# Weight loads on another queue, v ahead of them, and weight conversions placed between attention steps in a two-block kernel

## The chip, the cores and the metric

The kernel runs on one NeuronCore of a Trainium2 chip. The metric is device time in microseconds of one execution; several executions are timed and the median is given. A separate execution is recorded by the hardware profiler, and its span is slightly shorter than the timed value. Engine names are those of the profile: PE (TensorE matmul), PEld (its weight loads), DVE (VectorE), ACT (ScalarE), POOL (GpSimd), SP (SyncE, which here only issues transfers).

## The reference

Two blocks follow each other. The first is a gated recurrence per batch and head, the second a gated state-space block on its output. All inputs are float32 except where the harness hands over 64-bit floats for the weights; the kernel reads the weights as pairs of 32-bit words.

```python
# attention: B=4, H=8, S=768, D=48
for t in range(S):
    state = alpha[:, :, t, :, None] * state + einsum('bhd,bhe->bhde', k[:, :, t], v[:, :, t])
    y[:, :, t] = einsum('bhd,bhde->bhe', q[:, :, t], state)
x = y.transpose(0, 2, 1, 3).reshape(B, S, H * D)      # 384 wide
# second block: d_inner = 512
proj = x @ w_in                                        # 384 x 1024
val, gate = proj[..., :512], proj[..., 512:]
h = exp(A_log) * h + val[:, t]                         # scan over t
out = (silu(gate) * h) @ w_out                         # 512 x 384
```

## The kernel before

The function `fast` does the work; a second function, `general`, only runs if checks of the input ranges fail, and takes no part in the times. The sequence is cut into 12 groups of 256 rows (three for each of four batches), and each group into two chunks of 128. A group passes through two parts.

**Attention part.** Alpha is brought to a transposed layout (`natural_alpha` for the first three groups: PE transposes, ACT copies into `aT`). `products` scans alpha on DVE into cumulative products and their inverses. `natural_qk` transposes k and q on PE, and `times` multiplies them on DVE by inverse and product, into Z. `scores` are matmuls of Z with Z, `masks` multiplies them with a triangular mask (one half on DVE, the other copied by ACT and multiplied on POOL, tile A), `keys` transposes k back for the state. `state` accumulates the state of the recurrence in PSUM and ACT copies it to `S_sb`; `values` and `carried` make the output y from A and v, and from the state and Z. `join` copies y to xT on ACT and moves 16 rows of each head pair to their place by six small transfers within SBUF.

**Second part.** `project` makes, for each of four blocks of 128 inner channels, pv and pg from xT and `w_in`: six matmuls, each into a PSUM tile of a pool of three (`ps_mm`), which transposes and outputs share. `gated` scans pv on DVE into hh, applies Silu to pg on ACT (sg), and multiplies both on POOL (f). `output` multiplies f with `w_out`, and SP stores the result.

**Weights.** They arrive as two 32-bit words for each element. `load_w_in(half, engine)` loads half of w_in into partitions 64 x half and up, in two transfers (48 rows and 16 rows, 1152 and 384 KB). `load_w_out` takes two transfers of 768 KB. `convert(i)` turns the words into float32: ACT makes `wr` from the low words, DVE two operations from the high words, and the returned function adds wr on POOL. The first four conversions are the four blocks of w_in (each needs both halves of the load); conversions NI and NI + 1 are the two halves of w_out. The wr tiles come from a pool of two buffers.

**Order.** The program is written out by hand: each engine runs its instructions in the order in which the code issues them, and waits only on semaphores of what it needs. Transfers are issued from SP, ACT or POOL, each with a queue of its own in the profile: q1 is SP's, q10 is ACT's, q0 (named software_dynamic) is POOL's. In the prologue SP issues, in this order, alpha, k and q of group 0, alpha of group 1, v of group 0, k and q of group 1, half 0 of w_in, v of group 1, w_out, and then the inputs of groups 2 and 3. ACT issues half 1 of w_in after the copies of group 0's masks. Group 0 and group 1 go through attention before the main loop; the loop then projects group n while it computes attention of group n + 1 and the products of n + 2. For group 0 (`nat` is true only there) the two conversions of w_out stand after the second and the third projection.

The lines that matter around the change: L443 (transfers of w_in), L448 (w_out), L429 (v), L510 (wr on ACT), L511 and L513 (conversion on DVE), L515 (add on POOL), L557 (aT), L652 (mask on POOL), L685 and L688 (state and S_sb), L664 and L675 (values and carried), L698 (transfers of join), L713 (projection), L720, L725, L726 (hh, sg, f), L734 (output). Between the attention of group 1 and the loop, the code reads:

```python
    for i in range(NI):
        convert(i)()
    state(1, 0)
    values(1, 0)
    values(1, 1)
    state(1, 1)
    carried(1, 0)
    carried(1, 1)
    join(1, (nc.gpsimd, nc.gpsimd))
```

Of the kernel before, what the change touches and what calls it, by code (L numbers as in the profile page):

```python
# [346 lines left out]
def fast(  # L347
# [22 lines left out]
    C = 128  # L370
# [10 lines left out]
    def pool(name, bufs, **kw):  # L381
        return ctx.enter_context(tc.tile_pool(name=name, bufs=bufs, **kw))
# [2 lines left out]
    p1 = pool("p1", 1)  # L385
    p2 = pool("p2", 2)
    p3 = pool("p3", 3)
    ps_sc = pool("ps_sc", 2, space=PS)
    ps_st = pool("ps_st", 1, space=PS)
    ps_mm = pool("ps_mm", 3, space=PS)  # L390
# [35 lines left out]
    def load_v(m, engine, cs=range(G)):  # L426
        b, g = divmod(m, NG)
        for c in cs:
            engine.dma_start(out=vs[m % NV][:, c, :, 0:D],  # L429
                             in_=v[b, :, ds(g * GC + c * C, C), :].rearrange("h p d -> p h d"))  # L430
# [9 lines left out]
    def load_w_in(half, engine):  # L440

        for row, size, first, step in ((64 * half, D, 4 * half * D, D), (64 * half + D, R, (4 * half + 3) * D, R)):
            engine.dma_start(out=bits_in[ds(row, size)].rearrange("p kk n two -> p kk (n two)"),  # L443
                             in_=moe_w_in.bitcast(U32)[ds(first, NK * step)]
                             .rearrange("(kk p) n -> p kk n", p=step)[0:size])
# [51 lines left out]
    def convert(i):  # L497


        if i < NI:  # L500
            bits = bits_in.rearrange("p kk (vg n) two -> p kk vg n two", vg=2)[:, :, :, ds(i * C, C)]
            w = w_in[:, :, :, ds(i * C, C)]
        else:
            rows = ds(2 * (i - NI), 2)
            bits, w = bits_out[:, rows, None], w_out[:, rows, None, :]
        lo, hi = bits[..., 0], bits[..., 1]
        _, x, y, z = w.shape
        r = p2.tile([C, x, y, z], I32, tag="wr", name="wr")
        t = w.bitcast(U32)
        nc.scalar.activation(r, lo, AF.Copy, scale=2.0 ** -29)  # L510
        nc.vector.tensor_scalar(out=t, in0=hi, scalar1=3, scalar2=0x3FFFFFFF,  # L511
                                op0=ALU.logical_shift_left, op1=ALU.bitwise_and)
        nc.vector.scalar_tensor_tensor(out=t, in0=hi, scalar=0xC0000000, in1=t,  # L513
                                       op0=ALU.bitwise_and, op1=ALU.bitwise_or)
        return lambda: nc.gpsimd.tensor_tensor(out=w.bitcast(I32), in0=w.bitcast(I32), in1=r, op=ALU.add)  # L515
# [35 lines left out]
    def natural_alpha(m):  # L551

        for c in range(G):
            tp = ps_mm.tile([C, 4, C], FP32, tag="mm", name="tn")
            for p in range(4):
                nc.tensor.transpose(tp[:, p, :], natural("a", m)[:, c, 2 * p:2 * p + 2, :], ident)
            nc.scalar.activation(alphas[:, :, ds(c * C, C)], tp, AF.Copy)  # L557

    def natural_qk(m, name):

        if m not in Zs:
            Zs[m] = p2.tile([C, 4, 2, GC], FP32, tag="Z", name="Z")
        tps = []
        for c in range(G):
            tp = ps_sc.tile([C, 4, C], FP32, tag=f"sc{c}", name="tn")
            for p in range(4):
                nc.tensor.transpose(tp[:, p, :], natural(name, m)[:, c, 2 * p:2 * p + 2, :], ident)
            tps.append(tp)

        def times(c):  # L570
            i, by = {"k": (1, invs), "q": (0, prods)}[name]
            cols = ds(c * C, C)
            nc.vector.tensor_mul(Zs[m][:, :, i, cols], tps[c], by[:, :, cols])  # L573
        return times

    def check_alpha(m):

        if m < NAT:
            src = natural("a", m)[:, :, :, 0:D]
        else:  # L580
            src = raw_bufs[m % NR]["a"].rearrange("p h (j d) -> p h j d", d=D)[:, :, :, 0:32]
        _, x, y, z = src.shape
        junk = p1.tile([C, x, y, z], BF16, tag="junk", name="junk")
        nc.scalar.activation(junk, src, AF.Relu, bias=minus, accum_out=above[:, m:m + 1])
# [53 lines left out]
    def scores(m, c):  # L638
        Z = Zs[m]
        cols = ds(c * C, C)  # L640
        sc = [ps_sc.tile([C, 4, C], FP32, tag=f"sc{i}", name=f"sc{i}") for i in range(2)]
        for p in range(4):
            for i in range(2):
                rows = ds(64 * i, D)
                nc.tensor.matmul(sc[i][:, p, :], Z[rows, p, 1, cols], Z[rows, p, 0, cols], start=True, stop=True)  # L645
        As[m, c] = p2.tile([C, 2, 4, C], FP32, tag="A", name="A"), sc
# [43 lines left out]
    def join(m, engines):  # L690

        y = ys.pop(m)
        xT = xTs[m] = p2.tile([C, 4, GC], FP32, tag="xT", name="xT")
        nc.scalar.activation(xT[:, 1::2], y[1], AF.Copy)
        nc.scalar.activation(xT[:, 0::2], y[0], AF.Copy)
        for s in range(2):
            for a in range(NK):
                engines[s].dma_start(out=xT[ds(64 * s + D, R), a], in_=xT[ds(64 * s + R * a, R), 3])  # L698


    prev_h = [None] * NI
# [46 lines left out]
    def pair(name, m, one, other):  # L748
        load_natural(name, m, 0, one)
        load_natural(name, m, 1, other)  # L750
# [7 lines left out]
    load_v(0, SP)  # L758
    pair("k", 1, SP, SP)
    pair("q", 1, SP, SP)  # L760
    load_w_in(0, SP)
    load_v(1, SP)
    for i in range(2):
        load_w_out(i, SP)

    constants()

    al = ps_mm.tile([C, NI], FP32, tag="mm", name="al")
    nc.tensor.transpose(al, a_log, ident[0:NI, 0:NI])
    nc.scalar.activation(a_dec, al, AF.Exp)  # L770
    nc.scalar.activation(ok, start_p, AF.Silu)


    natural_alpha(0)
    check_alpha(0)
    k_times, q_times = natural_qk(0, "k"), natural_qk(0, "q")
    for name in "akq":
        pair(name, 2, SP, SP)

    def warm(count):  # L780

        t = ps_mm.tile([C, 4, C], FP32, tag="mm", name="warm")
        for _ in range(count):
            nc.tensor.matmul(t, ident, ident[:, None, :].to_broadcast([C, 4, C]), start=True, stop=True)

    warm(5)
    for _ in products(0):
# [3 lines left out]
        q_times(c)  # L791
    for c in range(G):
        scores(0, c)
    for c in range(G):
        masks(0, c)
    load_w_in(1, ACT)
    for c in range(G):
        keys(0, c)
    natural_alpha(1)
# [6 lines left out]
    values(0, 1)  # L806
    state(0, 1)
    carried(0, 1)
    join(0, (nc.gpsimd, nc.gpsimd))
    k_times, q_times = natural_qk(1, "k"), natural_qk(1, "q")  # L810
    warm(4)
    for _ in steps:
# [5 lines left out]
    for c in range(G):  # L818
        scores(1, c)
    for c in range(G):  # L820
        keys(1, c)
    for c in range(G):
        masks(1, c)
    for i in range(NI):
        convert(i)()
    state(1, 0)
    values(1, 0)
# [1 line left out]
    state(1, 1)  # L829
    carried(1, 0)  # L830
    carried(1, 1)
    join(1, (nc.gpsimd, nc.gpsimd))

    checks = itertools.chain.from_iterable(check_w(i) for i in range(NW))
    value = None
    for n in range(N):
        m = n + 1
        att = 0 < n < N - 1
        nat = n + 2 < NAT
        steps = products(n + 2) if n + 2 < N else iter(())  # L840

        def go(count):
            for _ in range(count):
                next(steps, None)


        if n + 3 < N:
            loads(n + 3)
        if n + 2 < N:
            load_v(n + 2, SP)  # L850

        def attend():
            for c in range(G):
                keys(m, c)
            for c in range(G):
                scores(m, c)


        pj = project(n, 0)
        gated(n, 0, *pj)  # L860
        if att:
            attend()
        if not nat:
            go(1)
        if att:
            for c in range(G):
                masks(m, c)
        pj = project(n, 1)
        gated(n, 1, *pj)
        if nat:  # L870
            natural_alpha(n + 2)
            check_alpha(n + 2)
            convert(NI)()
        else:
            go(1)
        pj = project(n, 2)
        gated(n, 2, *pj)
        if nat:
            convert(NI + 1)()
        else:  # L880
            go(2)
        if att:
            state(m, 0)
            values(m, 0)
            values(m, 1)
            state(m, 1)
            carried(m, 0)
            carried(m, 1)
            join(m, (SP, ACT))
        pj = project(n, 3)  # L890
        gated(n, 3, *pj)
        go(10)
        if 3 <= n:
            for _ in itertools.islice(checks, 2):
                pass
        if n == N - 2:
            check_end()
        if n == N - 1:
            value = nc.values_load(flag[0:1, 0:1], min_val=0, max_val=1)
        output(n)  # L900
        if nat:
            k_times, q_times = natural_qk(n + 2, "k"), natural_qk(n + 2, "q")
            for c in range(G):
                k_times(c)
                q_times(c)
# [39 lines left out]
```

## Time and profile before

| | before |
|---|---|
| time, median of 3 | 324.39 us (324.18 to 324.83) |
| span of the profiled execution | 321.5 us |
| PE busy | 290.4 us (90%) |
| PEld busy | 231.6 us (72%) |
| DVE busy | 227.2 us (71%) |
| POOL busy | 115.7 us (36%) |
| ACT busy | 97.1 us (30%) |
| moved by transfers | 39.71 MB, mean 124 GB/s |
| first projection matmul (L713) starts | 54.6 us |
| output of group 0 (L734) ends | 76.0 us |

Busy times are sums over the span and say nothing of where an engine waits. The profile also gives the chain of work that ended last (each step followed back to what released it), the waits by who waited for whom, the instructions in order of time, and the transfers by queue. The picture by time has two stretches: a prologue of some 77 us in which inputs and weights arrive and groups 0 and 1 go through attention, and a steady loop in which PE works on one group every 22 us.

### The profile page before, as it was taken

The page shows a single profiled execution, that of the slowest core. Times are in us where ns is not written, and L with a number is a line of the kernel's source. Part 1 is how long each engine was busy: PE and PEld are TensorE (multiplying, and loading weights), DVE is VectorE, ACT ScalarE, POOL GpSimd, SP SyncE. Part 2 cuts the span into 40 slices and gives each one's busy share as a digit, 9 for nine tenths or more (in the row PEclk, how much of TensorE's full clock was granted, in tenths as well). Part 3 has the DMA queues.
Part 4 walks back from the last instruction along what each step waited for, and adds up shares of the span by engine and source line. Part 5 has one row for each costly group of instructions (what it writes and reads, how often), then busy time and mean ns, then how long its engine had stood idle before and what let it go on. Part 6 is the DMA issues. An engine that isn't in the chain of part 4 may idle for free.

```text
span 321.5 us, 5980 instructions
## 1 busy us (share of the span) xinstructions
PE 290.4 (90%) x2349; PEld 231.6 (72%) x2349; DVE 227.2 (71%) x244; ACT 97.1 (30%) x200; POOL 115.7 (36%) x109
## 2 busy tenths in 40 slices
PE   2999145969999999999999999999999999999992
PEld 2585144847887878868868878788688688786771
DVE  3857057497896895998998998989979689432110
ACT  4261223321424225224214333251242143221211
POOL 6033327590640602804506207218043064150020
PEclk9999756999999999999999999999999999999999
DMA  9999999964935937908829439469089220100101
GB/s 131 163 157 159 138 249 178 231 83 113 233 45 135 224 42 190 191 13 210 175 75 248 79 105 234 62 169 206 18 217 167 66 46 10 54 1 14 49 5 56
DMA packets 66029, 39.71 MB, mean 124 GB/s; under 512 B 47044, under 2 KB 65096, under 8 KB 65608
## 3 DMA queue, kind: packets, MB, share of 16 engines
q1 hardware_dynamic: 63376, 36.78, 58.1%
q10 hardware_dynamic: 2232, 2.27, 4.4%
q8 instruction: 20, 0.33, 0.5%
q0 software_dynamic: 384, 0.20, 0.5%
q14 instruction: 17, 0.14, 0.1%
HBM read 33.33 MB, written 4.72 MB: 118 GB/s over the span
## 4 chain that ended last, share of the span: by engine, by line
PE 80%; DMA 9%; DVE 3%; POOL 3%; ACT 2%; issue 0%; ACTq 0%; DVEq 0%; POOLq 0%
PE pv L713 21%; PE o L734 19%; PE pg L713 19%; DMA bits_in<-in_moe_w_in_dram 8%; PE sc L645 7%; PE y L664 5%; PE y L675 3%; PE st L685 3%; PE tp L635 2%; DMA a_log<-in_moe_A_log_dram 1%; POOL w_in L515 1%; POOL w_out L515 1%; ACT wr L510 1%; DVE inv L611 1%; DVE prod L599 1%; DVE Z L573 1%
## 5 line engine op out<-in xcount | busy, mean ns | idle before, releaser
L726 POOL TENSOR_TENSOR f<-sg,hh 128x256 f32<-128x256 f32 x48 | 60.6, 1262 | 142.4 <-ACT sg L725 140.9
L713 PE MATMUL pv<-xT,w_in 128*128 128x256 f32 x288 | 73.5, 392 | 0.0
L713 PE MATMUL pg<-xT,w_in 128*128 128x256 f32 x288 | 70.0, 379 | 0.0
L734 PE MATMUL o<-w_out,f 128*128 128x384 f32 x192 | 64.4, 488 | 2.9 <-POOL w_out L515 2.9
L713 PEld LDWEIGHTS pv<-xT,w_in 128*128 128x128 f32 x288 | 53.6, 193 | 12.1 <-issue 2.2
L713 PEld LDWEIGHTS pg<-xT,w_in 128*128 128x128 f32 x288 | 54.9, 191 | 7.6
L734 PEld LDWEIGHTS o<-w_out,f 128*128 128x128 f32 x192 | 36.2, 190 | 26.4 <-POOL w_out L515 3.9
L725 ACT ACTIVATE sg<-pg 128x256 f32<-128x256 f32 x48 | 18.4, 384 | 102.5 <-PE pg L713 85.6
L720 DVE TENSOR_TENSOR_SCAN hh<-a_dec,hh,pv 128x256 f32<-128x256 f32 x32 | 23.5, 734 | 33.5 <-PE pv L713 31.6
L652 POOL TENSOR_TENSOR A<-A,mask 128x512 f32<-128x512 f32 x24 | 30.0, 1269 | 34.9 <-ACT A L651 34.9
L599 DVE TENSOR_TENSOR_SCAN prod<-aT,first 128x1024 f32<-128x1024 f32 x12 | 32.8, 2735 | 0.1
L611 DVE TENSOR_TENSOR_SCAN inv<-aT,last 128x1025 f32<-128x1025 f32 x12 | 29.4, 2450 | 0.4
L738 ACT ACTIVATE o_sb<-o 128x384 f32<-128x384 f32 x24 | 11.8, 491 | 51.9 <-PE o L734 51.9
L685 PE MATMUL st<-v,ktm 128*64 128x48 f32 x320 | 13.9, 232 | 14.3 <-DMA v<-in_v_dram 10.6
L645 PE MATMUL sc<-Z 48*128 48x128 f32 x384 | 25.5, 278 | 1.2 <-DVE Z L573 0.7
L645 PEld LDWEIGHTS sc<-Z 48*128 48x128 f32 x384 | 22.8, 188 | 4.9 <-issue 2.8
L685 PEld LDWEIGHTS st<-v,ktm 128*64 128x64 f32 x320 | 12.2, 146 | 18.1 <-issue 14.1
L664 PE MATMUL y<-A,v 128*64 128x128 f32 x384 | 24.4, 281 | 0.0
L720 DVE TENSOR_TENSOR_SCAN hh<-a_dec,pv 128x256 f32<-128x256 f32 x16 | 10.9, 681 | 16.1 <-PE pv L713 16.1
L653 DVE TENSOR_TENSOR A<-sc,mask 128x512 f32<-128x512 f32 x24 | 16.6, 692 | 7.9 <-PE sc L645 5.5
L664 PEld LDWEIGHTS y<-A,v 128*64 128x64 f32 x384 | 21.8, 142 | 0.2 <-issue 0.2
L590 DVE STREAM_TRANSPOSE aT<-raw_a 128x1024 f32<-128x1024 f32 x9 | 18.4, 2039 | 0.0
(86 smaller groups left out, 277.7 us busy)
## 6 DMA issues: line engine op xcount, KB each, us to landing
raw_k<-in_k_dram SPq DMA_DIRECT2D x24, 192.0 KB, 5.2
raw_q<-in_q_dram SPq DMA_DIRECT2D x24, 192.0 KB, 5.8
v<-in_v_dram SPq DMA_DIRECT2D x24, 192.0 KB, 4.5
out_dram<-o_sb SPq DMA_DIRECT2D x24, 192.0 KB, 1.9
raw_a<-in_alpha_dram SPq DMA_DIRECT2D x23, 192.0 KB, 3.9
raw_a<-in_alpha_dram SPq DMA_DIRECT2D x18, 176.0 KB, 4.1
raw_k<-in_k_dram SPq DMA_DIRECT2D x18, 176.0 KB, 5.2
raw_q<-in_q_dram SPq DMA_DIRECT2D x18, 176.0 KB, 4.9
```

The costliest lines, as they stand in the source:

```text
L590: nc.vector.transpose(out=to.rearrange("p h (c j) -> p h j c", j=NT), in_=raw_bufs[m % NR][name].rearrange("p h (j d) -> p h j d", d=D)[:, ...
L599: nc.vector.tensor_tensor_scan(out=prod, data0=aT[:, 0:4 * GC], data1=first.rearrange("p h n -> p (h n)"), initial=0.0, op0=ALU.mult, op1= ...
L611: nc.vector.tensor_tensor_scan(out=inv[:, ::-1], data0=aT[:, ::-1], data1=last.rearrange("p h n -> p (h n)")[:, 0:4 * GC + 1][:, ::-1], in ...
L645: nc.tensor.matmul(sc[i][:, p, :], Z[rows, p, 1, cols], Z[rows, p, 0, cols], start=True, stop=True)
L652: nc.gpsimd.tensor_mul(A[:, 1], A[:, 1], mb)
L664: nc.tensor.matmul(ys[m][i][ds(64 * s, 64), e, ds(c * C, C)], v_sb[:, c, 2 * p + i, :], A[:, i, p, :], start=(c == 0 and e == 0), stop=Fal ...
L685: nc.tensor.matmul(st[ds(64 * i, 64), p, :], ktms[c][:, p, i, :], vs[m % NV][:, c, 2 * p + i, 0:D], start=(ch == 0 and p == 0), stop=(ch = ...
L713: nc.tensor.matmul(pj, w_in[:, kk, vg, ds(cc * C, C)], xT[:, kk, :], start=(kk == 0), stop=(kk == NK - 1))
L720: nc.vector.tensor_tensor_scan(out=hh, data0=a_dec[:, cc:cc + 1].to_broadcast([C, GC]), data1=pv, initial=prev_h[cc][:, GC - 1:GC] if g el ...
L725: nc.scalar.activation(sg, pg, AF.Silu)
L726: nc.gpsimd.tensor_mul(fs[n][:, cc, :], sg, hh)
L734: nc.tensor.matmul(os[c], fs[n][:, cc, ds(c * C, C)], w_out[:, cc, :], start=(cc == 0), stop=(cc == NI - 1))
```

## The change

Half 1 of w_in is issued by POOL instead of ACT, at the same point of the program. On SP's queue v of group 1 goes ahead of half 0 of w_in. The conversions of the weights are spread: only the first two blocks of w_in are converted ahead of group 1's state and values, the other two after its xT has been copied and before POOL issues the join's transfers (`join` now returns the function that issues them), and the ACT and DVE parts of w_out's conversion move ahead of the loop, with POOL's adds left inside the first group's steps, the first one now directly after the second projection. The wr tiles get a pool of four buffers. Group 1's masks go ahead of its keys. At the start, PE gets three warming matmuls, alpha of group 0 is transposed ahead of A_log, and the dummy activations that load the function tables stand elsewhere (Exp first, Silu after the first scores). The purpose is to get the weights in on two queues at once and to keep w_in's arrival from holding up the second group's attention.

```diff
--- before.py
+++ after.py
@@ -385,6 +385,7 @@
     p1 = pool("p1", 1)
     p2 = pool("p2", 2)
     p3 = pool("p3", 3)
+    p4 = pool("p4", 4)
     ps_sc = pool("ps_sc", 2, space=PS)
     ps_st = pool("ps_st", 1, space=PS)
     ps_mm = pool("ps_mm", 3, space=PS)
@@ -505,7 +506,7 @@
             bits, w = bits_out[:, rows, None], w_out[:, rows, None, :]
         lo, hi = bits[..., 0], bits[..., 1]
         _, x, y, z = w.shape
-        r = p2.tile([C, x, y, z], I32, tag="wr", name="wr")
+        r = p4.tile([C, x, y, z], I32, tag="wr", name="wr")
         t = w.bitcast(U32)
         nc.scalar.activation(r, lo, AF.Copy, scale=2.0 ** -29)
         nc.vector.tensor_scalar(out=t, in0=hi, scalar1=3, scalar2=0x3FFFFFFF,
@@ -693,9 +694,12 @@
         xT = xTs[m] = p2.tile([C, 4, GC], FP32, tag="xT", name="xT")
         nc.scalar.activation(xT[:, 1::2], y[1], AF.Copy)
         nc.scalar.activation(xT[:, 0::2], y[0], AF.Copy)
-        for s in range(2):
-            for a in range(NK):
-                engines[s].dma_start(out=xT[ds(64 * s + D, R), a], in_=xT[ds(64 * s + R * a, R), 3])
+
+        def transfers():
+            for s in range(2):
+                for a in range(NK):
+                    engines[s].dma_start(out=xT[ds(64 * s + D, R), a], in_=xT[ds(64 * s + R * a, R), 3])
+        return transfers
 
 
     prev_h = [None] * NI
@@ -758,30 +762,30 @@
     load_v(0, SP)
     pair("k", 1, SP, SP)
     pair("q", 1, SP, SP)
+    load_v(1, SP)
     load_w_in(0, SP)
-    load_v(1, SP)
     for i in range(2):
         load_w_out(i, SP)
 
     constants()
-
+    def warm(count):
+
+        t = ps_mm.tile([C, 4, C], FP32, tag="mm", name="warm")
+        for _ in range(count):
+            nc.tensor.matmul(t, ident, ident[:, None, :].to_broadcast([C, 4, C]), start=True, stop=True)
+
+    nc.scalar.activation(ok[:, 0:1], minus, AF.Exp)
+    warm(3)
+
+
+    natural_alpha(0)
     al = ps_mm.tile([C, NI], FP32, tag="mm", name="al")
     nc.tensor.transpose(al, a_log, ident[0:NI, 0:NI])
     nc.scalar.activation(a_dec, al, AF.Exp)
-    nc.scalar.activation(ok, start_p, AF.Silu)
-
-
-    natural_alpha(0)
     check_alpha(0)
     k_times, q_times = natural_qk(0, "k"), natural_qk(0, "q")
     for name in "akq":
         pair(name, 2, SP, SP)
-
-    def warm(count):
-
-        t = ps_mm.tile([C, 4, C], FP32, tag="mm", name="warm")
-        for _ in range(count):
-            nc.tensor.matmul(t, ident, ident[:, None, :].to_broadcast([C, 4, C]), start=True, stop=True)
 
     warm(5)
     for _ in products(0):
@@ -791,9 +795,10 @@
         q_times(c)
     for c in range(G):
         scores(0, c)
+    nc.scalar.activation(ok[:, 0:1], minus, AF.Silu)
     for c in range(G):
         masks(0, c)
-    load_w_in(1, ACT)
+    load_w_in(1, nc.gpsimd)
     for c in range(G):
         keys(0, c)
     natural_alpha(1)
@@ -806,7 +811,7 @@
     values(0, 1)
     state(0, 1)
     carried(0, 1)
-    join(0, (nc.gpsimd, nc.gpsimd))
+    join(0, (nc.gpsimd, nc.gpsimd))()
     k_times, q_times = natural_qk(1, "k"), natural_qk(1, "q")
     warm(4)
     for _ in steps:
@@ -818,10 +823,10 @@
     for c in range(G):
         scores(1, c)
     for c in range(G):
+        masks(1, c)
+    for c in range(G):
         keys(1, c)
-    for c in range(G):
-        masks(1, c)
-    for i in range(NI):
+    for i in range(2):
         convert(i)()
     state(1, 0)
     values(1, 0)
@@ -829,7 +834,11 @@
     state(1, 1)
     carried(1, 0)
     carried(1, 1)
-    join(1, (nc.gpsimd, nc.gpsimd))
+    y1_out = join(1, (nc.gpsimd, nc.gpsimd))
+    for i in range(2, NI):
+        convert(i)()
+    y1_out()
+    w_out_sums = [convert(i) for i in (NI, NI + 1)]
 
     checks = itertools.chain.from_iterable(check_w(i) for i in range(NW))
     value = None
@@ -868,15 +877,15 @@
         pj = project(n, 1)
         gated(n, 1, *pj)
         if nat:
+            w_out_sums[0]()
             natural_alpha(n + 2)
             check_alpha(n + 2)
-            convert(NI)()
         else:
             go(1)
         pj = project(n, 2)
         gated(n, 2, *pj)
         if nat:
-            convert(NI + 1)()
+            w_out_sums[1]()
         else:
             go(2)
         if att:
@@ -886,7 +895,7 @@
             state(m, 1)
             carried(m, 0)
             carried(m, 1)
-            join(m, (SP, ACT))
+            join(m, (SP, ACT))()
         pj = project(n, 3)
         gated(n, 3, *pj)
         go(10)
```

## The prediction

> **What bounds the kernel now.** I read the chain that ended last first, in order of time. From 77.8 us to the end it is PE alone, one piece of matmuls on the next, about 22.2 us a group (o L734 begins at 94.34, 116.51, 139.12). Nothing in the diff touches that stretch, so what the change is worth is how much earlier or later PE gets there. Before it the chain is not PE:
>
> ```profile
> 18.70 24.94 DMA bits_in<-in_moe_w_in_dram
> 43.80 1.74 ACT wr L510 x2
> 45.53 2.01 POOL w_in L515
> 47.56 0.93 ACT wr L510
> 48.50 1.99 POOL w_in L515
> 50.51 0.90 ACT wr L510
> 51.40 0.23 ACT S_sb L688
> 51.68 1.09 PE st L685 x16
> 52.77 1.89 PE y L675 x32
> 54.66 2.85 PE pv L713 x6
> ...
> 68.09 3.75 POOL w_out L515
> 71.89 4.14 PE o L734 x12
> 76.03 1.75 PE tn L567 x16
> ```
>
> The columns are start, length, and work. Call T the moment w_in is there, 43.8 us. The first projection starts at T + 10.9, and the first output (o L734) ends at T + 32.2 = 76.0. The four copies wr sit on ACT ahead of S_sb, so PE cannot finish the second group's values until 51.7.
>
> Next the waits, and the issues with their time to landing: the second group's v is a cause of idleness too, but it comes at the same moment as w_in.
>
> ```profile
> PE st L685 <- DMA v<-in_v_dram: 10.6, 1, 10.6
> bits_in<-in_moe_w_in_dram ACTq DMA_DIRECT2D x1, 1152.0 KB, 23.1
> xT<-xT POOLq DMA_DIRECT2D x12, 16.0 KB, 9.2
> ```
>
> Last the transfers: busy time by stretch (the last two columns are the DMA share and GB/s), then the queue rows of 20 to 24 us (one) and of 30 to 31 us (two): packets, MB, share of 16 engines.
>
> ```profile
> 20.00:24.00 4.00, 4.00 (x86) 3.59 (x86) 2.47 (x3) 2.84 (x8) 0.69 (x1) 1.00 1.01 133
> 28.00:32.00 4.00, 3.64 (x34) 2.24 (x33) 2.34 (x5) 0.00 (x0) 0.47 (x1) 1.00 0.96 178
> ```
>
> ```profile
> q1 hardware_dynamic: 65, 0.53, 101.4%
> q10 hardware_dynamic: 14, 0.11, 62.7%
> q1 hardware_dynamic: 16, 0.10, 46.4%
> ```
>
> Alone, half 0 of w_in (SP's, q1) keeps all engines occupied at 133 GB/s: 65 packets of 8 KB in 4 us are 1.014 x 16 x 4 / 65 = 1.0 us each. Where both halves are in flight they make 0.21 MB in one us. ACT issued its half at 18.33, yet its queue q10 shows no packet before the stretch 27 to 28: the halves ran one after the other.
>
> [...] 133 GB/s for one half of w_in, but 1.50 MB in the 4 us from 44, mostly w_out over 128 partitions. [...] 210 against 133 GB/s in the us shown. [...] q10 waited some 9 us behind q1 before they alternated. [...]
>
> ```profile
> 44.43 0.96 DVE L513 SCALAR_TENSOR_TENSOR w_in<-bits_in,w_in 128x768 uint32<-128x768 uint32 x1
> 45.89 2.45 DVE L513 SCALAR_TENSOR_TENSOR w_in<-bits_in,w_in 128x768 uint32<-128x768 uint32 x1
> ```
>
> The second waited for the GpSimd add of 45.53 to 47.53, so a conversion costs 2.95 us once they follow each other.
>
> **The change part by part.**
>
> *Start of the kernel.* Three warm matmuls, an earlier transpose of alpha, table loads elsewhere. In before, alpha's copies on ACT began at 7.64 behind a 1.28 us table load; they may come up to 0.9 us earlier. The transfers hide this: T does not depend on it. It only brings the A masks on GpSimd (ended 20.7) to about 20.2, and with them the new w_in issue. The moved Silu load falls where ACT idles 7.67 us.
>
> *v ahead of w_in on SP.* Two transfers of 192 KB, 0.39 MB at the 163 GB/s of the stretch 12 to 16: 2.4 us before w_in's first packet, which moves from 18.3 to 20.7. In before these bytes moved mostly after 40 us, so T pays for them.
>
> *Half 1 on GpSimd's queue.* The cost hangs on x, when the first packet of that queue (q0) moves. I check the sum on before: half 0 alone from 18.3 to 27.6 at 0.133 MB/us is 1.24 MB; the other 0.33 MB of its 1.57 and as much of half 1 at 0.21 take 3.1 us, to 30.7; half 1's remaining 1.24 MB take 9.3, to 40.0; the tail to 43.8 is 3.8. In after, SP's queue holds w_out behind w_in, so while q0 is alone with it each packet of 1.0 us alternates with one of 3 KB, about 0.13 us (16 engines x 4 us over about 480): 13% more. The bounds of x come from GpSimd's own transfers: the join issued at 56.14 shows packets in 58 to 60, up to 3.4 us later: x = 23.6; the join at 25.38, behind w_in's packets, shows none before 33, and q10 waited 9.3 us after w_in's first packet: x = 30.
> - x = 23.6: 0.39 MB alone, 2.36 at 0.21 = 11.2 us, to 34.8; 0.39 alone 2.9 + 0.4; with the tail T = 41.9, 1.9 earlier. Were both at twice 133, T would be near 39.
> - x = 26.8: 0.81 alone, 1.52 together 7.2 us, to 34.0; 0.81 alone 6.1 + 0.8; T = 44.7, 0.9 later.
> - x = 30: before's course shifted by 2.4, plus 1.2: T = 47.4, 3.6 later.
>
> I take the middle, because neither end has been seen for such packets on this queue.
>
> *The second group's steps.* v has landed, so its first state and values matmuls run in PE's idle time before T: nothing. Now only two wr stand ahead of S_sb: S_sb at T + 1.8 and not 7.6, carried matmuls done by T + 5, xT copied by T + 6.4, wr 3 and 4 by T + 8.2. GpSimd's adds keep their rhythm (T + 1.7, 4.65, 7.6, 10.6, end 12.4), for VectorE sets it. The first projection starts at T + 5 (before: T + 10.9). But both w_out conversions now stand on VectorE ahead of the scans hh. The first waits for GpSimd's fourth add, so they end at T + 14.7, and hh of the first block follows. Queued behind that scan is PE: the second pg needs the buffer of the first pv (three mm buffers), so it starts at T + 15.5; before it started at 60.1 = T + 16.3. The early projection gains only 0.8.
>
> *w_out's conversion before the loop.* GpSimd's first w_out add waited for ACT at 64.9 and the second fell beside the long scan (3.78 us against 2.0 for a free add, both from the timeline); PE lost 2.9 us there. Now both have their inputs early: first add at T + 18.1 after f of the second block, second at T + 21.4 to 23.4, before the scan. PE runs through: 7.35 us from second pg to the end of the fourth (60.1 to 67.45 before), then 5.2 of output, T + 28.0 against T + 32.2: 4.2 us. PE, however, now idles some 5 us before that pg. After the idle time to 44 the granted clock was 0.5 and sixteen st took 1.10 us against 0.62 to 0.67 later; a clock at half over pg, tn and half of pv adds up to 2.2. So between 2.0 and 4.2; I take 3.1. Four wr buffers cost nothing: they only let ACT run ahead of GpSimd.
>
> *Sum:* +0.9 - 3.1 = -2.2, so 322.2.
>
> **The rivals.**
>
> *The halves truly side by side.* For it: 178 and 210 GB/s where they overlapped[...]. Against it: q10 also had its own queue and waited. T 1.9 to 4.8 earlier, with the 3.1 makes -5.0 to -7.9: about 318.
>
> *Slower: the software queue waits as ACT's did.* For it: the 8 us of GpSimd's first join, the same as q10's, which speaks for some eight packets of 8 KB already taken in by each engine. By the time q0 is ready, half 0 would be nearly all taken in. T is 3.6 later and PE comes back at half clock: +3.6 - 2.0 = +1.6, 326.0. With the clock kept, +0.5. Against it: half 0 starts later here and GpSimd issues slightly sooner.
>
> *w_out lands late.* It stands behind w_in on SP; if it came after T + 10.4, the scans would wait for it. At before's 375 GB/s it needs 4 us after q0 is done; I hold it for landed by T + 3, so it costs nothing. A delay to T + 13 would make the first case 324.8, no change.
>
> **How the numbers follow.** The middle 0.42, side by side 0.23, waiting queue 0.30, late w_out 0.05. Faster: 0.36 of the middle (its clock may be half) and all of 0.23, total 0.59. Within 0.65 us: 0.09, from the middle's worse end, late w_out and the kept clock. Slower: 0.32, the waiting queue and the worst of x. The range runs from 317.0 (short of the fastest overlap) to 326.4 (past the slow rival).
>
> **What would show it.** In the profile after: q0's first packet of w_in between 23 and 30 and GB/s above 200 while it overlaps q1; the first wr at 44.7; S_sb some 2 us after; the first pv long before the first hh, an idle PE until hh; no wait of o for w_out. If wr starts after 47, the queue waited; before 42, the halves ran together. If PE's second pg comes well before T + 15, my order on VectorE is wrong.

## The result and the profile after

| | before | after |
|---|---|---|
| time, median of 4 | 324.28 us (323.96 to 324.83) | 328.12 us (327.03 to 328.36) |
| ratio after / before | | 1.011, 95% interval 1.0083 to 1.0137 |
| span of the profiled execution | 321.5 us | 325.3 us |
| PE busy | 290.4 us | 294.9 us |
| w_in there (T, the first wr) | 43.8 us | 45.4 us |
| output of group 0 ends | 76.03 us | 76.79 us |
| from the output of group 1 to that of group 2 (start to start) | 22.17 us | 24.87 us |

The kernel became 3.8 us slower; 322.2 us was predicted. The time was lost in two places, more than 20 us apart. The chain that ended last in the kernel after (start, length, work):

```profile
20.68 24.66 DMA bits_in<-in_moe_w_in_dram
...
56.34 2.44 DVE w_out L514
60.97 2.93 PE pg L717 x6
63.90 1.71 PE tn L557 x8
65.61 2.13 PE pv L717 x6
71.63 5.16 PE o L738 x16
...
95.10 5.17 PE o L738 x16
100.80 1.92 issue
102.72 1.53 PE pv L717 x6
...
119.97 5.16 PE o L738 x16
```

Read it in three steps. **To 45.4:** w_in comes 1.6 us later. **To 76.8:** the wait for ACT's wr and for group 1's values is gone from the chain, and o no longer waits for w_out. In their place VectorE converts w_out (56.34), and only then scans; PE resumes at 60.97, and its pg takes 2.93 us. In before pg took 1.46 (its line is shown below). All that the spread conversions won is lost again: 0.8 us later than before. **From 95.1:** between the outputs of groups 1 and 2 stands an "issue" of 1.92 us that before doesn't have. It is the other 2.7 us: 119.97 - 95.10 = 24.87 against 116.51 - 94.34 = 22.17. From there on the two kernels run alike, 3.46 us apart; the last 0.3 lie behind the last output.

The second step in the waits (all engines), with what ended the wait, the sum in us, the number and the longest:

```profile
PE pg L717 <- DVE hh L724: 4.9, 1, 4.9
```

And the stretches around it; the third column from the right is the granted clock of PE, as a share of full speed:

```profile
60.00:64.00 4.00, 3.03 (x8) 2.38 (x9) 1.50 (x3) 0.06 (x1) 1.57 (x3) 0.54 1.11 227
64.00:68.00 4.00, 4.00 (x16) 3.55 (x15) 0.22 (x1) 2.44 (x5) 2.49 (x2) 0.60 1.12 150
```

After the 4.95 us without work PE runs at about half its clock, not for one piece but for pg, the transposes tn and most of pv. In before both stretches had clock 1.00, and the same pg (third line, from the timeline) took half as long:

```profile
60.00:64.00 4.00, 4.00 (x24) 3.59 (x23) 2.49 (x4) 2.48 (x6) 0.99 (x2) 1.00 1.10 233
64.00:68.00 4.00, 3.99 (x18) 3.09 (x18) 3.40 (x7) 2.40 (x5) 3.10 (x2) 1.00 1.25 178
59.94 1.46 PE L713 MATMUL pg<-xT,w_in 128*128 128x256 f32 x6
```

The third step shows on SP, which does no arithmetic and which the chain therefore hides under "issue". SP's instructions in order of time, after (start, length of the group; the transfers are counted at the end):

```profile
79.75 3.32 SPq L406 DMA_DIRECT2D raw_k<-in_k_dram  x4
83.48 13.24 SPq L406 DMA_DIRECT2D raw_q<-in_q_dram  x4
96.77 1.23 SPq L430 DMA_DIRECT2D v<-in_v_dram  x2
98.33 2.45 SPq L701 DMA_DIRECT2D xT<-xT  x3
```

and the same stretch before:

```profile
80.89 4.48 SPq L405 DMA_DIRECT2D raw_q<-in_q_dram  x4
85.73 1.92 SPq L429 DMA_DIRECT2D v<-in_v_dram  x2
94.66 1.88 SPq L698 DMA_DIRECT2D xT<-xT  x3
```

Four loads of q for group 4 took 4.48 us to issue before and 13.24 now. Behind them stand SP's three join transfers of group 2, which the next projection needs; they leave at 98.33, 4.8 us after ACT's three of the same join (93.52). SP's own list of waits names whom it waited for:

```profile
SPq L406 <- DMA xT<-xT: 11.7, 1, 11.7
```

A load of q needs nothing of xT. By time it stood for ACT's three transfers of the join: in after ACT issued them from 93.52 on, they took 1.8 to 1.9 us to land, and SP went on at 95.46. In e7 and e8 below the same two moments are 90.50 and 92.36, and 95.92 and 97.79: each time 1.9 us from ACT's first issue to SP's next load. In before SP's loads of this stretch are out by 87.7, and what waits for xT is SP's own first transfer of the join, which leaves at 94.66, behind ACT's (92.76 on); SP's list for 76 to 126 us, with two joins in it:

```profile
SPq L698 <- DMA xT<-xT: 12.3, 2, 6.7
```

So with half 1 of w_in off ACT, loads stand for data with which they have nothing to do. I call this the false wait. The runs sort by the engine that issues half 1. Where ACT does, no load of q waits for xT in SP's list (before, e2, e4 and e6 below). Where POOL does, a load of q waits for it, for 11.7 us in after, 11.6 in e3, 8.8 in e7 and up to 11.9 in e8, unless group 2's half of the join leaves ACT as well (e1, e5). By what mechanism a load of SP's stands for transfers of ACT's, and why the queue of half 1 decides it some 60 us later, the traces do not show.

The transfers of w_in, first by issue (KB, us to landing), then the queues of 30 to 31 us:

```profile
bits_in<-in_moe_w_in_dram POOLq DMA_DIRECT2D x1, 1152.0 KB, 22.1
```

```profile
q1 hardware_dynamic: 15, 0.11, 57.0%
q0 software_dynamic: 9, 0.07, 36.9%
```

POOL issued its half at 19.9; q0's first packets show between 29 and 30. In 22 to 24 us q1 alone made 32 packets, 0.26 MB, much as half 0 did before (35 packets). The halves overlap from there at 178 to 188 GB/s (windows of 2 us from 30 to 36), not at 210.

### The profile page after: what moved, and what is told of

Its sections match the earlier page's. It is cut to its first block, busy times and chain, and to the rows that moved or that the text cites. A ratio compares the mean times of both kernels' runs of the same rounds, so it can differ in the third digit from the quotient of the medians.

```text
span 325.3 us, 5997 instructions
## 1 busy us (share of the span) xinstructions
PE 294.9 (91%) x2355; PEld 232.6 (71%) x2355; DVE 227.4 (70%) x244; ACT 97.4 (30%) x201; POOL 114.2 (35%) x111
## 4 chain that ended last, share of the span: by engine, by line
PE 80%; DMA 9%; DVE 5%; SPq 1%; POOL 1%; issue 1%; ACT 0%; DVEq 0%; POOLq 0%
PE pv L717 20%; PE o L738 19%; PE pg L717 19%; DMA bits_in<-in_moe_w_in_dram 8%; PE sc L646 7%; PE y L665 5%; PE y L676 3%; PE st L686 3%; DVE w_in L514 3%; PE tp L636 2%; DMA raw_q<-in_q_dram 2%; PE warm L775 1%; SPq L421 1%; DVE w_out L514 1%; POOL A L653 1%
## 5 line engine op out<-in xcount | busy, mean ns | idle before, releaser
L717 PE MATMUL pv<-xT,w_in 128*128 128x256 f32 x288 | 74.5, 396 | 2.5 <-issue 2.5
L717 PE MATMUL pg<-xT,w_in 128*128 128x256 f32 x288 | 71.7, 386 | 4.9 <-DVE hh L724 4.9
L717 PEld LDWEIGHTS pg<-xT,w_in 128*128 128x128 f32 x288 | 55.8, 194 | 13.2 <-DVE hh L724 5.3
L717 PEld LDWEIGHTS pv<-xT,w_in 128*128 128x128 f32 x288 | 54.3, 195 | 15.1 <-issue 5.2
L653 POOL TENSOR_TENSOR A<-A,mask 128x512 f32<-128x512 f32 x24 | 30.0, 1271 | 31.3 <-ACT A L652 31.3
L665 PE MATMUL y<-A,v 128*64 128x128 f32 x384 | 23.4, 274 | 0.0
L665 PEld LDWEIGHTS y<-A,v 128*64 128x64 f32 x384 | 20.8, 137 | 0.2 <-issue 0.2
```

The costliest lines, as they stand in the source:

```text
L653: nc.gpsimd.tensor_mul(A[:, 1], A[:, 1], mb)
L665: nc.tensor.matmul(ys[m][i][ds(64 * s, 64), e, ds(c * C, C)], v_sb[:, c, 2 * p + i, :], A[:, i, p, :], start=(c == 0 and e == 0), stop=Fal ...
L717: nc.tensor.matmul(pj, w_in[:, kk, vg, ds(cc * C, C)], xT[:, kk, :], start=(kk == 0), stop=(kk == NK - 1))
```

## The experiments

The experiments' times spread more than those above (kernel before: 321.4 to 328.1 us but for two single executions of 355 and 1680 us, medians 324.3 to 324.5), so ratios to it are given with their 95% intervals. The columns ahead of the last are each from one profiled execution, which need not be typical: e2's took 320.36 us, e4's 323.51, e1's 326.3. They are: T, when the output of group 0 ends, the difference of the two, and the distance between the outputs of groups 1 and 2.

| run | T | group 0 ends | after T | groups 1 to 2 | median us, ratio to before |
|---|---|---|---|---|---|
| before | 43.8 | 76.0 | 32.2 | 22.17 | |
| after | 45.4 | 76.8 | 31.4 | 24.87 | 328.1, 1.011 |
| e1 join on POOL | 47.3 | 78.6 | 31.3 | 22.17 | 324.30, 1.0006 (0.9975 to 1.0036) |
| e2 half 1 on ACT | 43.3 | 73.2 | 29.9 | 22.18 | 325.19, 1.0040 (1.0011 to 1.0069) |
| e3 w_out in the steps | 44.5 | 70.7 | 26.2 | 26.26 | 323.55, 0.9959 (0.9930 to 0.9987) |
| e4 before, v first | 43.9 | 75.7 | 31.8 | 22.17 | 325.82, 1.0019 (0.9982 to 1.0056) |
| e5 e3 and e1 | 45.1 | 71.3 | 26.2 | 22.17 | 320.09, 0.9883 (0.9796 to 0.9969) |
| e6 ACT after keys | 43.6 | 69.8 | 26.2 | 22.17 | 318.04, 0.9822 (0.9735 to 0.9910) |
| e7 PE kept busy | 45.4 | 73.8 | 28.4 | 22.75 | 322.62, 0.9945 (0.9917 to 0.9973) |
| e8 before, POOL's queue | 44.9 | 79.2 | 34.3 | 25.61 | 331.33, 1.0236 (1.0136 to 1.0336) |
| e9 small transfers | 43.1 | 69.2 | 26.2 | 22.17 | 318.88, 0.9848 (0.9775 to 0.9920) |
| e10 one queue | 49.1 | 75.3 | 26.2 | 22.17 | 322.46, 0.9934 (0.9909 to 0.9960) |

**e1, the false wait taken away.** Only group 2's half of the join leaves ACT.

```diff
-            join(m, (SP, ACT))()
+            join(m, (SP, nc.gpsimd if m == 2 else ACT))()
```

> The changed kernel, except that for group 2 alone the second three transfers of the join are issued by POOL instead of ACT[...]. Theory (false wait): of the 3.8 us lost, 2.7 come from SP standing from 83.5 to 95.5 us before a load of q, until ACT's transfers of the join landed; SP's own join transfers then came at 98.3 instead of 94.7 and the projection of group 2 waited 2.5 us. Without it SP does not stand there, the first pv of group 2 starts within 0.3 us of the end of the output before it, and the time is 325.4. Rival (the load itself is late, because the transfers as a whole run later): the wait at 100.3 stays and the time is 328.

SP no longer stands, and 22.17 us lie between the outputs again. The second pg of group 0 is as slow as in after, in start, length, then in brackets the idle time before and who ended it:

```profile
62.83 2.93 PE L717 MATMUL pg<-xT,w_in 128*128 128x256 f32 x6 [5.00 <-DVE hh L724]
```

The median is that of before: by the ratios 1.0% under the kernel after, and 1.1 us under what was expected. So the false wait is a cause by itself. In this profile's list no load of q waits for xT, where one did for 11.7 us in after. This execution's T of 47.3 comes from the same prologue as after's 45.4: with half 1 on POOL's queue T ranged from 44.5 to 47.3 in the profiles of five kernels (after, e1, e3, e5, e7).

**e2, half 1 back on ACT's queue.**

```diff
-    load_w_in(1, nc.gpsimd)
+    load_w_in(1, ACT)
```

> The changed kernel with half 1 of w_in issued by ACT again, at the same point of the program; v stays ahead. Theory (taken in ahead): an engine takes in some eight packets of 8 KB before it alternates, so what counts is whether the second queue is ready before half 0 starts to move (20.7 us); ACT's issue, near 18.5[...], is; q10 should show packets of w_in from about 20 us, the halves overlap from the start, w_in is there at about 40 us instead of 45.4, and with the false wait gone too the time is about 320. Rival (transfers of SP and ACT are made up in the order of their issue, and q10 waits until SP's earlier ones are through): q10 starts near 30, w_in is there at 45 to 46, only the false wait goes, and the time is 325.4.

Neither picture was right. The halves did not overlap early, yet T is 43.3: now q10 went first and alone (in 22 to 24 us 32 packets and nothing on q1), and q1's half 0 came in the stretch 26 to 28. The queue whose packets of w_in come first is alone for some 6 to 9 us, whichever it is (q1 in before and after, q10 here). The false wait is gone too. The time decides nothing: the median met the rival's number without the rival's T, while the profiled execution was the fastest of twenty (320.36 us), near the theory's number. In that one PE's slow stretch cost 1.5 us and not 3.0 (T + 29.9 against T + 31.4), after an idle time of 4.79 us.

**e3, w_out's conversion back inside the steps.** Everything else as in after.

```diff
-    w_out_sums = [convert(i) for i in (NI, NI + 1)]
...
-            w_out_sums[0]()
             natural_alpha(n + 2)
             check_alpha(n + 2)
+            convert(NI)()
...
-            w_out_sums[1]()
+            convert(NI + 1)()
```

> The changed kernel with both conversions of w_out back where they were (ACT, DVE and POOL parts after the second and third projection of group 0). Theory (order on DVE and PE's clock): the scan hh of the first block follows w_in's fourth conversion, about 10.5 us after w_in is there instead of 14.8; PE's second pg starts at 56.5 instead of 61.0, its idle time is 2 us and the clock stays up, and the output of group 0 ends some 3 to 4 us earlier, in part given back to w_out's adds on POOL: 324.5 to 325.5. Rival (POOL's adds are what holds, wherever they stand): the output of group 0 waits for w_out's second add as in the kernel before, and the time stays within 1 us of 328.

The median came under both expectations. PE's instructions of group 0:

```profile
55.62 1.56 PE L717 MATMUL pg<-xT,w_in 128*128 128x256 f32 x6 [0.28 <-DVE hh L724]
...
66.58 4.14 PE L738 MATMUL o<-w_out,f 128*128 128x384 f32 x12 [1.61 <-POOL w_out L516]
```

The second pg starts at T + 11.1 instead of T + 15.6 and at full clock; o waits 1.6 us for w_out, and group 0 still ends at T + 26.2, 5.2 earlier than in after. So converting w_out ahead of the loop costs 5.2 us there, though it removes a wait of 2.9: 3.0 us are the clock, as e7 shows, and the other 2.2, by difference, the order on VectorE. The kernel doesn't get these 5.2 whole, because here the false wait takes 4.1 (26.26 - 22.17): PE reaches it earlier, stands 2.15 us and comes back at clock 0.67 (96 to 100 us).

**e4, v ahead of w_in, in the kernel before.**

```diff
-    load_w_in(0, SP)
     load_v(1, SP)
+    load_w_in(0, SP)
```

> The kernel before with v of group 1 ahead of half 0 of w_in on SP and nothing else; half 1 stays on ACT. Theory (taken in ahead): half 0 starts to move at 20.7 instead of 18.3, ACT's issue at 18.3 is now ready before it, the halves overlap from the start, w_in is there at about 40 us instead of 43.8, and the time is 320 to 321. Rival (made up in the order of issue): half 1 waits behind half 0 as before, everything shifts by v's 2.4 us, w_in is there at 46.2, and the time is 326.7.

It does nothing that can be measured, and neither picture came true: T is 43.9 against 43.8. v's bytes delay half 0, q10 goes first in its place (32 packets in 22 to 24 us, 2 small ones on q1), and the sum is the same.

**e5, e3 and e1 together.**

> The changed kernel with both suspected costs taken away: w_out's conversion back inside the first group's steps, and the second half of the third group's join (m = 2) issued by GpSimd instead of ScalarE[...]. Theory (clock and false wait are separate terms and add up): SyncE no longer stands behind xT, the third group's first pv follows o without a gap, the second pg of the first group takes 1.5 us and not 2.9; about 3 to 4 us less than with w_out's conversion back alone (323.55), so 319.5 to 320.5. Rival (both edits take away the same wait, or PE finds another one in the third group): no better than either alone, 323.5 to 324.3.

As the theory said: 320.09. T + 26.2, and 22.17 us after group 1. The two causes add up.

**e6, half 1 on ACT's queue, after the first keys.** As e3, with the issue moved.

```diff
-    load_w_in(1, nc.gpsimd)
     for c in range(G):
         keys(0, c)
+    load_w_in(1, ACT)
```

> The changed kernel with w_out's conversion back inside the steps and half 1 of w_in on ScalarE's queue, issued after the keys of the group's first chunk, so that it gets ready at about the moment at which SyncE's half 0 starts (20.7 us). Theory A (each transfer engine takes in some eight packets of the queue that is ready first, and alternates from the start if both get ready together): q1 and q10 both move from 21 to 22 us on at over 170 GB/s, w_in is there at 38 to 41 us, and the time is 315 to 318. Theory B (whichever is first by any margin is taken in alone for 8 us): one queue alone until 28 to 29, w_in there at 43.5 to 45, and 319 to 321. In both, SyncE doesn't stand behind xT in the third group.

Issued at 18.1, q10 was there first, and alone again; the queues of 22 to 23 us show a single row:

```profile
q10 hardware_dynamic: 17, 0.14, 107.9%
```

So it went as theory B has it, with w_in at 43.6; the time, 318.04, is 1 us better than B's range, at the border of A's, so that the packets decide here and not the time. It has the lowest median of all kernels here.

**e7, PE kept busy.** Five matmuls without use, ahead of the second pg of group 0 in the kernel after.

```diff
         for vg, pj in enumerate((pv, pg)):
+            if n == 0 and cc == 1 and vg == 1:
+                t = ps_sc.tile([C, 4, C], FP32, tag="sc0", name="fill")
+                for _ in range(5):
+                    nc.tensor.matmul(t, ident, ident[:, None, :].to_broadcast([C, 4, C]), start=True, stop=True)
```

> The changed kernel with five more matmuls without use on PE (of the warming kind, some 0.9 us each) ahead of the second pg of the first group, where PE idles 4.95 us until VectorE's scan. Theory (the half clock after this idle time is what the first group loses): pg takes 1.5 us and not 2.9, pg to the output's start takes 7.4 us and not 10.6, and the output of group 0 ends some 3 us earlier; the third group's standing SyncE is still there, so that the gain shows at the end only if that wait moves along with PE: 324.5 to 326 against 328.1 for the changed kernel. Rival (the clock is throttled for another reason, such as the DMA or the matmuls that went before): pg still takes 2.9 us and the time is 328 or slightly more.

PE's instruction, and the stretch of 60 to 64 us:

```profile
60.99 1.56 PE L721 MATMUL pg<-xT,w_in 128*128 128x256 f32 x6 [0.93 <-DVE hh L728]
```

```profile
60.00:64.00 4.00, 3.07 (x19) 2.73 (x19) 1.51 (x3) 1.33 (x3) 2.54 (x5) 1.00 1.09 220
```

pg starts where it did (60.99 against 60.97), at clock 1.00, and the output starts at 68.61 and not 71.63. So the half clock costs 3.0 us. The median is lower than expected by 2, because the false wait shrank as well, to 0.58 us: one load of q comes behind the wait (at 92.36) and not three (from 95.46 on), SP's xT transfers leave 3.6 us after ACT's instead of 4.8, and PE's work behind ACT's issue (until 97.2) nearly covers them.

**e8, the queue alone, in the kernel before.**

```diff
-    load_w_in(1, ACT)
+    load_w_in(1, nc.gpsimd)
```

> The kernel before with one edit: half 1 of w_in issued by GpSimd instead of ScalarE. Theory: w_in is there at 43 to 45 us as before (q0's packets come some 8 us after q1's, as q10's did), and the edit's cost comes from the third group, where SyncE's loads now stand behind ScalarE's join transfers: o of the third group starts some 3 us later, 326.5 to 328.5 in all. Rival (the standing SyncE needs the later first group to hurt, or belongs to the spread conversions): 324 to 325.

This one edit costs at least as much as the whole change: 331.33. The false wait is there (3.4 us), and T is 44.9, within the theory's 43 to 45. The time is 3 us above the theory's range. What the theory did not have is group 0's output, here ahead of the same line of before:

```profile
73.54 5.66 PE L734 MATMUL o<-w_out,f 128*128 128x384 f32 x12 [2.87 <-POOL w_out L515]
71.89 4.14 PE L734 MATMUL o<-w_out,f 128*128 128x384 f32 x12 [2.87 <-POOL w_out L515]
```

The same twelve matmuls after the same 2.87 us of idle time took 4.14 in before; here PE came back slow, with 5.66, and lost 1.5 us.

**e9, small transfers.** As e6 with e1's join; each half in four transfers of 16 rows.

```diff
-        for row, size, first, step in ((64 * half, D, ...), (64 * half + D, R, ...)):
+        for row, o, first, step in ((64 * half, 0, ...), (64 * half, R, ...),
+                                    (64 * half, 2 * R, ...), (64 * half + D, 0, ...)):
```

> As the kernel with half 1 on ScalarE after the first keys and w_out's conversion inside the steps (318.04, w_in there at 43.6 us, half 0 first seen 6 us after half 1), the third group's join on SyncE and GpSimd; and each half of w_in is now loaded in four transfers of 16 rows (3 packets of 8 KB for each of 16 engines) and not in two of 48 and 16 rows (9 and 3 packets). Theory A (an engine stays with one queue for as long as its share of one transfer lasts, nine packets so far): q1's packets of w_in begin some 3 us after q10's, w_in is there at 40 to 41.5 us, and the time is 315 to 316.5. Theory B (an engine has taken in some eight packets of the first queue, whatever transfers they are from): q1's begin 6 us after q10's as before, w_in at 43.5, time 317.5 to 319.

The queues of 22 to 23 us:

```profile
q1 hardware_dynamic: 11, 0.09, 53.6%
q10 hardware_dynamic: 9, 0.07, 44.1%
```

With 3 packets instead of 9 for each engine, both queues move in the same us, so the long stretch on one queue hangs on how the half is cut into transfers (theory A, and within 1 us rather than 3). The number of rows and their split changed together, so size alone is not proven. But the time doesn't follow: w_in is there at 43.1, and 318.88 can't be told from e6. From 22 to 40 us the engines moved 161 GB/s in the mean, and e6, with its long stretch on one queue, moved 160 in the same time: what the halves gain by an early overlap is not there in the sum. Side by side was never worth what the fast microsecond of before suggested.

**e10, both halves on one queue, piece by piece.**

```diff
-    load_w_in(0, SP)
+    for part in range(4):
+        for half in range(2):
+            load_w_in(half, SP, part)
...
-    load_w_in(1, ACT)
```

> As the kernel with four transfers of 16 rows for each half, but both halves issued by SyncE on its one queue, the pieces of the two halves in turn. Theory A ([...]pieces of both halves overlap where engines run apart or work on several packets): above 170 GB/s from 22 us on, w_in there at 37 to 40 us, 311.5 to 315. Theory B (one queue works its transfers one after the other on all engines[...]): 133 GB/s for all of w_in, there at 44.5 to 46 us, 319 to 321.

The stretch of 24 to 28 us; the last column is GB/s:

```profile
24.00:28.00 4.00, 3.79 (x20) 2.36 (x19) 3.86 (x5) 0.77 (x2) 2.92 (x6) 1.00 1.03 131
```

One queue stays at 131 GB/s here, and moved 125 in the mean from 22 to 40 us: taking the pieces in turn on one queue gave no overlap. T is later than theory B said (49.1 against 46 at most); where those 3 us come from is open.

## Why the prediction was wrong

**Steps that held.** The order on VectorE: S_sb at T + 1.6 (predicted T + 1.8), the first pv at T + 4.9 (T + 5), the second pg at T + 15.6 (T + 15.5). o no longer waits for w_out. GpSimd's first masks ended at 19.9 (20.2). With the clock kept (e7) group 0 ends at T + 28.4, where the prediction had T + 28.0. The rival of a late w_out did not come about.

**The size of the clock term.** "a clock at half over pg, tn and half of pv adds up to 2.2. So between 2.0 and 4.2; I take 3.1": that is 1.1 us for the clock, a middle value without a reason. The bound was summed wrongly, too: by the lengths in before, 1.29 + 0.87 + 0.65 is 2.8, and 2.2 holds pg and tn alone. e7 measured 3.0, with pv at 2.13 us still slowed over most of it. Of the 4.2 expected with the clock kept e7 shows 3.8; less 3.0, the gain in group 0 was 0.8 and not 3.1. What a loss costs is not fixed: after's gap of 4.95 us cost these 3.0, and e2's profile paid 1.5 us after a gap of 4.79. Nor do the runs show a sharp border in the length of the gap: one of 2.15 us lost the clock in e3 (0.67 in 96 to 100 us) and one of 2.46 in after didn't (1.00 in 100 to 104 us).

**"Nothing in the diff touches that stretch."** This failed outright, at 2.7 us. The prediction asked what an edit waits for by data and by buffers, and had no term for a load of one engine that stands until another engine's transfers have landed. e1 takes the wait away alone, and e8 brings it in with the one edit of the queue. That an engine "waits only on semaphores of what it needs", as the description of the kernel before has it, does not hold for the load of q that stood 11.7 us.

**When q0 moves.** x was 29 and not the middle 26.8, close to the slow end. T came 1.6 us later, where +0.9 was taken. The queue did this: v ahead left T at 43.9 (e4), POOL's queue alone put it at 44.9 (e8). But a single profile places T only roughly, by the spread from 44.5 to 47.3 above. The arithmetic was too pessimistic, for between its last two points x = 29 would give T = 46.6 against the 45.4 measured. The reading behind it failed too: I took the two ends of x from delays of 3.4 and 9.3 us in before and did not ask how a half is cut into transfers. 48 rows of three pieces of 8 KB on 16 engines are nine pieces for each, some 9 us at the 1.0 us a piece that before's 65 packets in 4 us give; that is an estimate, and about as long as the second queue stood. e9, with three pieces for each, has both queues at work within 1 us. That an engine works the nine as one is not shown.

**The sum.** Predicted, from T and group 0: +0.9 - 3.1 = -2.2. Measured in the profiles: T +1.6, group 0 after T -0.8, the false wait +2.7, behind the last output +0.3: +3.8. The rival of a waiting queue (326.0) was nearest, with a larger T and a smaller clock loss than came about; the rest of the distance is the false wait, which no rival had.

The diff's good part is probably the spread of w_in's conversions, which no run tries alone (v alone, e4, leaves 31.8): with w_out's conversion left in the steps and no false wait, group 0 ends 26.2 us after w_in is there in e5, e6, e9 and e10, against 32.2 before. That makes e6 faster than both kernels.

## What to carry to other kernels

An instruction moved out of the way of one wait lands ahead of something else on its own engine: look up who is queued behind it (here the scans), and price PE's restart after the new gap, not the gap alone. When a transfer moves to another queue, look in the profile for what every later transfer of the issuing engines waited for, even 60 us on (here POOL's issue at 19.9 and SP's wait from 83.8 to 95.5). Before two loads are credited with running side by side, look whether the second gets in before the first is through, and take the overlapped rate from a stretch of several microseconds.

## What the runs showed of the hardware

- The queue whose packets of w_in came first had the transfer engines to itself for about 6 to 9 us with transfers of nine 8 KB pieces an engine (before, after, e2, e4, e6); with three pieces both moved in the same us (e9, 22 to 23 us: 11 packets on q1, 9 on q10).
- Halves of w_in moved at 131 to 133 GB/s in stretches of 4 us with one queue at work (before 20 to 24 us; after and e10 24 to 28 us), on two queues, with whatever else was queued, at 135 to 208 GB/s in the stretches of 2 us from 30 to 36 us (after, e2, e6, e9). The mean from 22 to 40 us was 125 GB/s on one queue (e10) and 159 to 164 on two (after, e2, e6, e9).
- A load on SP that needs nothing of xT stood 8.8 to 11.9 us for ACT's transfers of xT where POOL issued half 1 of w_in (after, e3, e7, e8), and none did where ACT issued it (before, e2, e4, e6).
- PE's clock after a short gap is not a function of the gap alone: 2.15 us lost it (e3, 0.67), 2.46 us kept it (after, 1.00), and after 2.87 us the same twelve matmuls of o took 4.14 us in before and 5.66 in e8. A gap of 4.79 to 5.00 us lost it each time (after, e1, e2: six matmuls of pg in 2.93 us, 1.46 in before). A restart cost between 1.5 us (e2 and e8) and 3.0 us (after against e7).
